# An attention and two-MLP kernel on one core: a split first token block, and low word bits on ScalarE

## The chip, the cores and the metric

The kernel runs on one core of a Trainium2 chip. The metric is device time in microseconds (us), as the median of several runs. The core's engines are called by the names that the profile uses: PE is TensorE's matmul (PEld its weight load), DVE is VectorE, ACT is ScalarE, POOL is GpSimd, and SP is SyncE, which issues the DMA transfers here.

## What is computed

```
# attention: q, k, v float32 [4, 8, 768, 64]; mem_k, mem_v [4, 8, 8, 64]; 24 chunks of 32 queries
k_full = concat(mem_k, k[chunk start - 16 : chunk end + 8])      # clipped at the ends of the sequence
a = exp(s - max(s)),  s = (q_c @ k_full.T) / 8;  a = a / (sum(a) + 1e-9);  out_c = a @ v_full
x = out as [3072 tokens, 512]
# first MLP, weights float64: w_gate, w_val [512, 1536], w_out [1536, 512]
y = (sigmoid(x @ w_gate) * (x @ w_val)) @ w_out
# second MLP, weights float64: w_in [512, 2048], w_out [2048, 512]
h = y @ w_in;  result = (h * sigmoid(1.702 * h)) @ w_out
```

The weights arrive as float64 and are read as pairs of 32-bit words. The two MLPs work with every operand split into a high and a low part in the fp32r format, and each product is the sum of three: high by high, high by low, low by high.

## The kernel before

The 3,072 tokens are worked in six blocks of 512. Attention is cut into 32 tiles of 96 tokens (three chunks each). Tiles 0 to 4 and the first 32 tokens of tile 5 make up block 0; the rest of tile 5 and tiles 6 to 10 (the first 64 tokens of tile 10) make up block 1.

A tile of blocks 0 and 1 goes through these steps, by line: transposes of q and k on PE (L378, L386), copies out of the bank on ACT (L393 to L408), scores on PE (L495), maximum and subtraction on DVE (L512, L515), the exponential on ACT (L523), sum, small add and reciprocal on DVE (L552 to L555), the normalisation into `pw` in three 32-row pieces and one for the memory keys (L563, by DVE or POOL as the list `en` says), transposes of `pw` on PE (L585), copies out on DVE and ACT (L593, L595), the product with v on PE (L645), and last the split into x: the high part `xh` on ACT (L672) and the low part `xl` on DVE (L675). In tiles 0 to 5 (`early`) DVE normalises two pieces and POOL one; in later tiles DVE one and POOL two.

A weight chunk of 128 by 512 is made by `convert`: a 512 KB load, `rebias` on ACT (L257: the high words, scaled, as float32), `rest` on DVE (L262: the low words shifted right by 29), `sign` (the sign bit into the upper half of the low word: on ACT for even chunks, L267, on DVE for odd ones, L271), `join` on DVE (L276), `high` on ACT (L281: the high part of the split) and `low` on POOL (L285). The 36 chunks of the first MLP come first, three per step f (gate, val, out); the 32 chunks of the second MLP come between 600 and 750 us.

For each block the loop over f runs 12 steps: 12 matmuls of the gate (L726 high, L733 low), 12 of val, the gating (sigmoid on ACT L750, product on DVE L753, high part on ACT L756, low part L760), and, one step late, 12 matmuls of the output product (`gemm2`, L897), summed over all steps in four banks. A matmul here has 128 by 128 weights and 512 columns, and each has a weight load of its own.

All instructions are put in order by a planner when the program is written (`Schedule`): each task has an engine, an assumed duration, reads, writes, and a due time that falls back from its successors; at every point the planner takes, for the engine that is free first, the ready task with the earliest due time. Each engine then runs its list strictly in that order. The list `clock` holds the plan's time for products; it begins at 34 us, and tiles 0 to 4 with the first part of tile 5 are due 3 us apart up to that time, while tiles 6 to 10 have no due time of their own.

Of the kernel before, what the change touches and what calls it, by code (L numbers as in the profile page):

```python
# [8 lines left out]
F32 = mybir.dt.float32  # L9
# [3 lines left out]
F16 = mybir.dt.float16  # L13
# [6 lines left out]
CH = 32  # L20
# [102 lines left out]
def c_act(n):  # L123
    return 0.13 + n / 1200.0
# [7 lines left out]
def kernel(  # L132
# [69 lines left out]
    def xkeys(i):  # L202
        return [("x", i, c, o) for c in range(NCH) for o in range(2)]
# [27 lines left out]
    def convert(slot, src, gate=None):  # L231
# [27 lines left out]
        def rest():  # L259

            lo = words()[:, :, 0]
            nc.vector.tensor_scalar(out=lo, in0=lo, scalar1=29, scalar2=None, op0=ALU.logical_shift_right)  # L262

        def sign():

            half = bits().bitcast(F16).rearrange("p (c w) -> p c w", w=4)
            nc.scalar.activation(half[:, :, 1], words()[:, :, 1].bitcast(F32), AF.Copy, scale=2.0**-60)  # L267

        def sign_dve():
            half = bits().bitcast(U16).rearrange("p (c w) -> p c w", w=4)  # L270
            nc.vector.tensor_scalar(  # L271
                out=half[:, :, 1], in0=half[:, :, 3], scalar1=0x8000, scalar2=None, op0=ALU.bitwise_and
            )
# [17 lines left out]
        add("dve", 0.45, rest, r=[kr], w=[kr2])  # L291
        if u % 2:
            add("dve", 0.9, sign_dve, r=[kr], w=[kr2])
        else:
            add("act", 1.4, sign, r=[kr], w=[kr2])
        add("dve", 0.9, join, r=[kr, kr2], w=[kf])
# [38 lines left out]
    held_back = []  # L335
    SL = 0.5

    def attention(t, bufs, banks, pe_path, extra=None):
# [31 lines left out]
        if pe_path:  # L370
# [23 lines left out]

            early = t < NPRO
# [171 lines left out]
        if pe_path:  # L567
# [9 lines left out]
            en = ["dve", "dve" if early else "pool", "pool"]  # L577
            for c in range(NCK):
                tadd(en[c], 0.6 if en[c] == "dve" else 0.95, lambda c=c: ev_norm(c), r=ke + [kk["sm"]], w=[(kk["pw"], c)])
# [73 lines left out]
        def evict(part=None):  # L653

            g = range(t * NCK, (t + 1) * NCK)
            for i, blk in enumerate(sorted({c // NCH for c in g})):
# [7 lines left out]
                due = clock[0] - 3.0 * (NPRO - 1 - t) if t < NPRO and blk == 0 else None  # L664
# [54 lines left out]
    def first_product(slot, xb, n, bk, load=1.0):  # L719
        ts = [slice(t * P, (t + 1) * P) for t in range(NK)]  # L720

        def high():
            w = slots[slot]
            for t in range(NK):
                for x in (xhs, xls):
                    nc.tensor.matmul(  # L726
                        bank[bk][:, :n], w[:, 0, ts[t]], x[xb][:, t, :n], start=t == 0 and x is xhs, stop=False
                    )

        def low():  # L730
            w = slots[slot]
            for t in range(NK):
                nc.tensor.matmul(  # L733
                    bank[bk][:, :n], w[:, 1, ts[t]], xhs[xb][:, t, :n], start=False, stop=t == NK - 1
                )

        product(c_mm(n, 2 * NK), high, [("w", slot, 0)] + xkeys(xb), [("bank", bk)], load)
        product(c_mm(n, NK), low, [("w", slot, 1)] + xkeys(xb), [("bank", bk)], load)
# [46 lines left out]
    pro_banks = [(A0, A1), (Y[0], Y[1]), (Y[2], Y[3]), (G, V), (A0, A1), (Y[0], Y[1])]  # L785
# [104 lines left out]
    def gemm2(b, f, i, n):  # L890
        gh, gl = ghs[i], gls[i]

        def part(wi, g, j):
            def fn():
                w = slots[2 * F1 + f]
                for m in range(NK):
                    nc.tensor.matmul(  # L897
                        bank[Y[m]][:, :n],
                        w[:, wi, m * P : (m + 1) * P],
                        g[:, :n],  # L900
                        start=f == 0 and j == 0,
# [52 lines left out]
    LOAD = 1.12  # L954
    pend = None
    for b in range(NB):
# [5 lines left out]
        for f in range(F1):  # L962
            first_product(f, b % 2, n, G, LOAD)
            i, tail = gated(n, G, 1.0, V, b == 0 or b == NB - 1)
            first_product(F1 + f, b % 2, n, V, LOAD)
            tail()
            if pend:
                gemm2(*pend)
            pend = (b, f, i, n)
# [113 lines left out]
```

## Time and profile before

| what | value |
|---|---|
| median of 3 runs (lowest, highest) | 1261.01 us (1260.43, 1263.02) |
| the profiled execution, its own time | 1264.35 us |
| its span, first to last instruction | 1262.6 us |
| PE busy | 1231.8 us (98%) |
| DVE busy | 620.2 us (49%) |
| ACT busy | 475.0 us (38%) |
| POOL busy | 236.0 us (19%) |
| mean granted clock of TensorE | 0.989 |

The profiled execution took 1264.35 us, of which 1.75 us lie outside the span, and it is 3.3 us above the median of the runs. Busy shares are means over the whole span. A busy PE is one with a matmul under way; matmuls overlap, so that the time from one start to the next says what one costs, and not its own length.

### The profile page before, as it was taken

How to read it: one execution, taken by the hardware profiler on the slowest of the kernel's cores; microseconds unless marked ns; L12 is line 12 of the kernel's file. 1: busy time of each engine (PE TensorE's matmuls, PEld its weight loads, DVE VectorE, ACT ScalarE, POOL GpSimd, SP SyncE). 2: the span in 40 equal slices, each digit the busy share in tenths (PEclk: the TensorE clock that was granted, in tenths of full speed). 3: DMA queues.
4: the chain of work that ended last, by engine and by line, in shares of the span. 5: the costliest groups of instructions: out<-in, count | busy, mean ns of one | idle time of the engine just before them, and what ended most of it. 6: DMA issues, size and time to landing. Idle time of an engine off the chain costs nothing.

```text
span 1262.6 us, 18066 instructions
## 1 busy us (share of the span) xinstructions
PE 1231.8 (98%) x7120; PEld 987.7 (78%) x7120; DVE 620.2 (49%) x1161; ACT 475.0 (38%) x754; POOL 236.0 (19%) x198
## 2 busy tenths in 40 slices
PE   7799899999999999999999999999999999999998
PEld 5677777777777887787788788888888888888886
DVE  6979852786488528816677711122322222222322
ACT  4687742342244224313576632222222222322212
POOL 2465740010000001000365642110010000100000
PEclk9699999999999999999999999999999999999999
DMA  9556522223022202400365410010100200100000
GB/s 205 147 164 179 136 57 67 41 49 69 18 52 49 63 10 49 94 2 18 118 186 157 132 67 1 17 50 1 50 17 1 67 1 1 67 1 1 34 1 34
DMA packets 166036, 78.03 MB, mean 62 GB/s; under 512 B 132542, under 2 KB 153278, under 8 KB 165950
## 3 DMA queue, kind: packets, MB, share of 16 engines
q1 hardware_dynamic: 165950, 76.87, 23.5%
q8 instruction: 56, 0.92, 0.3%
q14 instruction: 30, 0.25, 0.1%
HBM read 64.24 MB, written 12.58 MB: 61 GB/s over the span
## 4 chain that ended last, share of the span: by engine, by line
PE 90%; DVE 5%; DMA 1%; ACT 1%; issue 1%; POOL 1%; SPq 1%; DVEq 0%; POOLq 0%; ACTq 0%
PE bank L726 33%; PE bank L704 21%; PE bank L733 17%; PE bank L897 14%; PE bank L645 2%; PE bank L495 1%; DVE f L276 1%; DVE pw L563 1%; SPq L305 1%; POOL pw_a L563 1%; PE bank L585 0%; DVE raw_s L262 0%; DVE raw L271 0%; DVE raw L262 0%; DVE sm L552 0%
## 5 line engine op out<-in xcount | busy, mean ns | idle before, releaser
L726 PE MATMUL bank<-xh,w 128*128 128x512 f32 x960 | 382.4, 398 | 2.3 <-ACT w L281 2.0
L726 PE MATMUL bank<-xl,w 128*128 128x512 f32 x960 | 380.9, 397 | 0.0
L753 DVE TENSOR_TENSOR sig<-bank,sig 128x512 f32<-128x512 f32 x168 | 115.9, 690 | 434.1 <-ACT sig L750 337.3
L733 PE MATMUL bank<-xh,w 128*128 128x512 f32 x960 | 264.1, 398 | 0.0
L750 ACT ACTIVATE sig<-bank 128x512 f32<-128x512 f32 x168 | 100.6, 599 | 389.6 <-PE bank L733 389.3
L704 PE MATMUL bank<-w,gh 128*128 128x512 f32 x768 | 241.0, 395 | 0.0
L726 PEld LDWEIGHTS bank<-xh,w 128*128 128x128 f32 x960 | 181.5, 189 | 47.9 <-ACT w L281 2.3
L726 PEld LDWEIGHTS bank<-xl,w 128*128 128x128 f32 x960 | 181.5, 189 | 43.3
L733 PEld LDWEIGHTS bank<-xh,w 128*128 128x128 f32 x960 | 179.3, 188 | 42.8
L756 ACT ACTIVATE gh<-sig 128x512 fp32r<-128x512 f32 x168 | 106.2, 632 | 197.4 <-DVE sig L753 190.3
L704 PEld LDWEIGHTS bank<-w,gh 128*128 128x128 f32 x768 | 144.6, 188 | 33.7
L897 PE MATMUL bank<-gh,w 128*128 128x512 f32 x576 | 159.6, 399 | 0.0
L704 PE MATMUL bank<-w,gl 128*128 128x512 f32 x384 | 151.1, 393 | 0.0
L897 PEld LDWEIGHTS bank<-gh,w 128*128 128x128 f32 x576 | 108.5, 190 | 26.5 <-DVE f L918 0.2
L760 DVE TENSOR_TENSOR gl<-sig,gh 128x512 fp32r<-128x512 f32 x128 | 91.0, 711 | 74.5 <-ACT gh L756 74.2
L285 POOL TENSOR_TENSOR w<-f,w 128x512 fp32r<-128x512 f32 x68 | 96.2, 1428 | 62.7 <-ACT w L281 61.1
L563 POOL TENSOR_TENSOR raw<-e,sm 96x448 f32<-96x448 f32 x21 | 21.6, 1029 | 410.8 <-DVE sm L555 410.8
L704 PEld LDWEIGHTS bank<-w,gl 128*128 128x128 f32 x384 | 72.2, 188 | 17.1
L946 POOL TENSOR_TENSOR xl<-f,xh 128x512 fp32r<-128x512 f32 x24 | 31.4, 1318 | 279.9 <-ACT xh L943 279.9
L897 PE MATMUL bank<-gl,w 128*128 128x512 f32 x288 | 79.7, 398 | 0.0
L620 DVE STREAM_TRANSPOSE pt<-raw 32x256 f32<-32x256 f32 x168 | 73.1, 435 | 2.6
L760 POOL TENSOR_TENSOR gl<-sig,gh 128x512 fp32r<-128x512 f32 x40 | 55.7, 1391 | 73.3 <-ACT gh L756 68.7
(84 smaller groups left out, 908.6 us busy)
## 6 DMA issues: line engine op xcount, KB each, us to landing
raw<-in_moe_w_out_dram SPq DMA_DIRECT2D x24, 512.0 KB
raw<-in_moe_w_in_dram SPq DMA_DIRECT2D x16, 512.0 KB
y_dram<-f SPq DMA_DIRECT2D x24, 256.0 KB
f<-y_dram SPq DMA_DIRECT2D x24, 256.0 KB
out_dram<-f SPq DMA_DIRECT2D x23, 256.0 KB
vn<-in_v_dram SPq DMA_DIRECT2D x24, 240.0 KB
raw<-in_moe_w_gate_dram SPq DMA_DIRECT2D x8, 512.0 KB
raw<-in_moe_w_val_dram SPq DMA_DIRECT2D x8, 512.0 KB
```

What stands on the lines that cost most here:

```text
L285: nc.gpsimd.tensor_tensor(out=w[:, 1, :], in0=ft, in1=w[:, 0, :].bitcast(F32), op=ALU.subtract)
L563: eng.tensor_tensor(out=dst, in0=e3()[r, :, c], in1=T["sm"][r].to_broadcast([n, H, keys[1] - keys[0]]), op=ALU.mult)
L620: nc.vector.transpose(T["pt"][r * CH : (r + 1) * CH, :, c * CH : (c + 1) * CH], T["pn"][c * CH : (c + 1) * CH, :, kb * CH : (kb + 1) * CH],)
L704: nc.tensor.matmul(ps_out, a, c, start=(first and i == 0 and j == 0), stop=(last and i == n - 1 and j == 2),)
L726: nc.tensor.matmul(bank[bk][:, :n], w[:, 0, ts[t]], x[xb][:, t, :n], start=t == 0 and x is xhs, stop=False)
L733: nc.tensor.matmul(bank[bk][:, :n], w[:, 1, ts[t]], xhs[xb][:, t, :n], start=False, stop=t == NK - 1)
L750: nc.scalar.activation(sig[:, :n], bank[src_sig][:, :n], AF.Sigmoid, scale=scale)
L753: nc.vector.tensor_tensor(out=sig[:, :n], in0=bank[src_val][:, :n], in1=sig[:, :n], op=ALU.mult)
L756: nc.scalar.activation(gh[:, :n], sig[:, :n], AF.Copy)
L760: eng.tensor_tensor(out=gl[:, :n], in0=sig[:, :n], in1=gh[:, :n].bitcast(F32), op=ALU.subtract)
L897: nc.tensor.matmul(bank[Y[m]][:, :n], w[:, wi, m * P : (m + 1) * P], g[:, :n], start=f == 0 and j == 0, stop=f == F1 - 1 and j == 2,)
L946: nc.gpsimd.tensor_tensor(out=xls[xb][:, m, :], in0=st[:, :BLK], in1=xhs[xb][:, m, :].bitcast(F32), op=ALU.subtract)
```

## The change

The low word bits move to ACT: `rest` becomes an ACT instruction that reads the upper 16 bits of the low word as an unsigned number, scales it by 7.5/65536 and adds 2^23, so that the three bits stand at the foot of the written word. `sign` is now always DVE's, for every chunk, and ACT's form of it goes away. In tiles 0 to 5 DVE normalises one piece and POOL two, as in the later ones. The first block begins with f = 0 and f = 1 for its first 384 tokens (tiles 0 to 3), then does both steps for the other 128 tokens, and goes on with f = 2 at 512. Tiles 0 to 3 are due 3 us apart up to 34 us, tile 4 and the first part of tile 5 at 40 and 46 us, and tiles 6 to 10 are spread over 95 us after that clock value. Tile 5 uses the banks A0 and A1 in place of two of the output's. Some durations that the planner assumes are new.

```diff
 def c_act(n):
-    return 0.13 + n / 1200.0
+    return 0.2 + n / 1100.0
...
-    def xkeys(i):
-        return [("x", i, c, o) for c in range(NCH) for o in range(2)]
+    def xkeys(i, c0=0, n=BLK):
+        return [("x", i, c, o) for c in range(c0 // CH, (c0 + n) // CH) for o in range(2)]
...
         def rest():
-            lo = words()[:, :, 0]
-            nc.vector.tensor_scalar(out=lo, in0=lo, scalar1=29, scalar2=None, op0=ALU.logical_shift_right)
+            half = bits().bitcast(U16).rearrange("p (c w) -> p c w", w=4)
+            nc.scalar.activation(
+                words()[:, :, 0].bitcast(F32), half[:, :, 1], AF.Copy, scale=7.5 * 2.0**-16, bias=2.0**23
+            )
         def sign():
-            half = bits().bitcast(F16).rearrange("p (c w) -> p c w", w=4)
-            nc.scalar.activation(half[:, :, 1], words()[:, :, 1].bitcast(F32), AF.Copy, scale=2.0**-60)
-        def sign_dve():
             half = bits().bitcast(U16).rearrange("p (c w) -> p c w", w=4)
             nc.vector.tensor_scalar(
                 out=half[:, :, 1], in0=half[:, :, 3], scalar1=0x8000, scalar2=None, op0=ALU.bitwise_and
...
-        add("dve", 0.45, rest, r=[kr], w=[kr2])
-        if u % 2:
-            add("dve", 0.9, sign_dve, r=[kr], w=[kr2])
-        else:
-            add("act", 1.4, sign, r=[kr], w=[kr2])
-        add("dve", 0.9, join, r=[kr, kr2], w=[kf])
+        add("act", c_act(512), rest, r=[kr], w=[kr2])
+        add("dve", 0.95, sign, r=[kr], w=[kr2])
+        add("dve", 0.85, join, r=[kr, kr2], w=[kf])
...
+    SPREAD = 95.0
...
-            en = ["dve", "dve" if early else "pool", "pool"]
+            en = ["dve", "pool", "pool"]
             for c in range(NCK):
-                tadd(en[c], 0.6 if en[c] == "dve" else 0.95, lambda c=c: ev_norm(c), r=ke + [kk["sm"]], w=[(kk["pw"], c)])
+                tadd(en[c], 0.75 if en[c] == "dve" else 1.2, lambda c=c: ev_norm(c), r=ke + [kk["sm"]], w=[(kk["pw"], c)])
...
-                due = clock[0] - 3.0 * (NPRO - 1 - t) if t < NPRO and blk == 0 else None
+                due = None
+                if t < 4:
+                    due = clock[0] - 3.0 * (3 - t)
+                elif t < NPRO and blk == 0:
+                    due = clock[0] + 6.0 * (t - 3)
+                elif t < NPE and blk <= 1:
+                    due = clock[0] + SPREAD * (t - NPRO + 1) / (NPE - NPRO)
...
-    pro_banks = [(A0, A1), (Y[0], Y[1]), (Y[2], Y[3]), (G, V), (A0, A1), (Y[0], Y[1])]
+    pro_banks = [(A0, A1), (Y[0], Y[1]), (Y[2], Y[3]), (G, V), (A0, A1), (A0, A1)]
...
+    NEARLY, NFIRST = 2, 4 * TQ
...
-        for f in range(F1):
-            first_product(f, b % 2, n, G, LOAD)
-            i, tail = gated(n, G, 1.0, V, b == 0 or b == NB - 1)
-            first_product(F1 + f, b % 2, n, V, LOAD)
+        steps = [(f, 0, n) for f in range(F1)]
+        if b == 0:
+            steps[:NEARLY] = [(f, c, m) for c, m in ((0, NFIRST), (NFIRST, n - NFIRST)) for f in range(NEARLY)]
+        for f, c0, m in steps:
+            first_product(f, b % 2, m, G, LOAD, c0)
+            i, tail = gated(m, G, 1.0, V, b == 0 or b == NB - 1)
+            first_product(F1 + f, b % 2, m, V, LOAD, c0)
             tail()
             if pend:
                 gemm2(*pend)
-            pend = (b, f, i, n)
+            pend = (b, f, i, m, c0)
```

`first_product` and `gemm2` take the first column `c0` and write or read the columns from there on.

## Rows read from the trace of the kernel before

**Rows 1.** Stretches: length; busy us of PE, PEld, DVE, ACT, POOL; clock; DMA share, GB/s.

```profile
...
0.00:49.17 49.17, 32.00 (x481) 26.52 (x481) 37.56 (x79) 23.54 (x51) 14.22 (x23) 0.85 0.68 146
49.17:54.88 5.71, 5.71 (x14) 4.45 (x14) 5.68 (x6) 3.59 (x6) 4.21 (x3) 0.50 1.13 285
...
49.17:187.35 138.18, 128.77 (x852) 101.72 (x853) 109.93 (x160) 99.98 (x156) 84.96 (x70) 0.95 0.57 151
187.35:1262.00 1074.65, 1071.08 (x5789) 859.48 (x5787) 472.72 (x924) 351.52 (x548) 136.81 (x105) 1.00 0.18 47
...
```

**Rows 2.** Waits of TensorE (PE), 49.17 to 187.35 us: total us, times, longest.

```profile
...
PE bank L585 <- POOL pw_a L563: 6.2, 3, 3.2
...
```

**Rows 3.** VectorE (DVE) in order of time, 27 to 49 us: start, length, instruction.

```profile
...
27.74 1.89 DVE L563 TENSOR_TENSOR pw<-e,sm 32x448 f32<-32x448 f32 x2
...
43.34 0.76 DVE L262 TENSOR_SCALAR raw<-raw 128x512 int32<-128x512 int32 x2
...
44.88 0.73 DVE L271 TENSOR_SCALAR raw<-raw 128x512 uint16<-128x512 uint16 x1
...
48.72 0.69 DVE L276 SCALAR_TENSOR_TENSOR f<-f,raw 128x512 int32<-128x512 int32 x1 [0.26 <-ACT raw L267]
...
```

**Rows 4.** PE in order of time: pieces between 49 and 185 us.

```profile
...
49.17 0.79 PE L726 MATMUL bank<-xh,w 128*128 128x512 f32 x1 [2.04 <-ACT w L281]
49.76 0.63 PE L726 MATMUL bank<-xl,w 128*128 128x512 f32 x1
...
54.02 0.63 PE L726 MATMUL bank<-xl,w 128*128 128x512 f32 x1
...
81.19 0.88 PE L645 MATMUL bank<-pt,vn 128*64 128x96 f32 x16
...
86.21 0.60 PE L386 MATMUL bank<-ident_a,qkn_a 128*128 128x128 f32 x4
...
102.87 0.88 PE L585 MATMUL bank<-ident_a,pw_a 96*128 96x96 f32 x8 [1.20 <-POOL pw_a L563]
...
182.69 0.39 PE L726 MATMUL bank<-xh,w 128*128 128x512 f32 x1
...
184.32 0.40 PE L726 MATMUL bank<-xl,w 128*128 128x512 f32 x1
...
```

**Rows 5.** DVE by line and shape, 0 to 49.17 us: busy us, mean ns, idle before.

```profile
...
L563 DVE TENSOR_TENSOR pw<-e,sm 32x448 f32<-32x448 f32 x12 | 10.7, 893 | 0.3
L512 DVE TENSOR_REDUCE mx<-bank 96x4 f32<-96x256 f32 x12 | 4.7, 411 | 2.5 <-PE bank L495 2.4
L515 DVE TENSOR_TENSOR e<-bank,mx 96x256 f32<-96x256 f32 x12 | 4.5, 412 | 0.1
L552 DVE TENSOR_REDUCE sm<-e 96x8 f32<-96x512 f32 x6 | 4.0, 674 | 0.0
...
```

**Rows 6.** The same view for GpSimd (POOL).

```profile
...
L563 POOL TENSOR_TENSOR pw<-e,sm 32x448 f32<-32x448 f32 x6 | 7.0, 1170 | 28.3 <-ACT qt L393 13.1 <-DVE sm L555 10.1 <-DVE sm L554 5.2
...
```

**Rows 7.** Groups of DVE by line and shape, 49.17 to 187.35 us.

```profile
...
L262 DVE TENSOR_SCALAR raw<-raw 128x512 int32<-128x512 int32 x21 | 17.6, 844 | 5.6 <-DMA raw<-in_moe_w_out_dram 5.1 <-DMA raw<-in_moe_w_val_dram 0.6
L262 DVE TENSOR_SCALAR raw_s<-raw_s 128x512 int32<-128x512 int32 x10 | 12.9, 1290 | 0.0
L271 DVE TENSOR_SCALAR raw<-raw 128x512 uint16<-128x512 uint16 x11 | 12.1, 1097 | 0.1
...
L271 DVE TENSOR_SCALAR raw_s<-raw_s 128x512 uint16<-128x512 uint16 x5 | 5.7, 1139 | 0.1
...
```

**Rows 8.** The same view and stretch for ScalarE (ACT).

```profile
...
L267 ACT ACTIVATE raw<-raw 128x512 f16<-128x512 f32 x10 | 13.7, 1371 | 0.0
L257 ACT ACTIVATE f<-raw 128x512 f32<-128x512 f32 x21 | 13.6, 671 | 0.0
...
```

**Rows 9.** DVE in order of time, at 78.76 us.

```profile
...
78.76 2.77 DVE L262 TENSOR_SCALAR raw_s<-raw_s 128x512 int32<-128x512 int32 x1
```

**Rows 10.** POOL in order of time, at 77.44 us.

```profile
...
77.44 2.55 POOL L285 TENSOR_TENSOR w<-f,w 128x512 fp32r<-128x512 f32 x2
...
```

More of the change, by code (lines that the diff above doesn't have):

```diff
@@ L12 @@
 I64 = mybir.dt.int64
-F16 = mybir.dt.float16
 U16 = mybir.dt.uint16
@@ L393, in ev_q @@
                 nc.scalar.activation(T["qt"].rearrange("p a b -> p (a b)"), b0[:, : NP * TQ], AF.Copy)
-            early = t < NPRO
             def ev_k():
@@ L717, in product, with first_product @@
         clock[0] += dur * load
-    def first_product(slot, xb, n, bk, load=1.0):
+    def first_product(slot, xb, n, bk, load=1.0, c0=0):
         ts = [slice(t * P, (t + 1) * P) for t in range(NK)]
@@ L726, in high @@
                     nc.tensor.matmul(
-                        bank[bk][:, :n], w[:, 0, ts[t]], x[xb][:, t, :n], start=t == 0 and x is xhs, stop=False
+                        bank[bk][:, :n], w[:, 0, ts[t]], x[xb][:, t, c0 : c0 + n], start=t == 0 and x is xhs, stop=False
                     )
@@ L733, in low @@
                 nc.tensor.matmul(
-                    bank[bk][:, :n], w[:, 1, ts[t]], xhs[xb][:, t, :n], start=False, stop=t == NK - 1
+                    bank[bk][:, :n], w[:, 1, ts[t]], xhs[xb][:, t, c0 : c0 + n], start=False, stop=t == NK - 1
                 )
-        product(c_mm(n, 2 * NK), high, [("w", slot, 0)] + xkeys(xb), [("bank", bk)], load)
-        product(c_mm(n, NK), low, [("w", slot, 1)] + xkeys(xb), [("bank", bk)], load)
+        product(c_mm(n, 2 * NK), high, [("w", slot, 0)] + xkeys(xb, c0, n), [("bank", bk)], load)
+        product(c_mm(n, NK), low, [("w", slot, 1)] + xkeys(xb, c0, n), [("bank", bk)], load)
     ng = [0]
@@ L888, in attention_b, with gemm2 @@
             attention(t, x, (A0, A1), False, (0 if head else NCK, 2 - t % 2 if head else 0, first or t % TPB == 0))
-    def gemm2(b, f, i, n):
+    def gemm2(b, f, i, n, c0):
         gh, gl = ghs[i], gls[i]
@@ L897, in fn @@
                     nc.tensor.matmul(
-                        bank[Y[m]][:, :n],
+                        bank[Y[m]][:, c0 : c0 + n],
                         w[:, wi, m * P : (m + 1) * P],
                         g[:, :n],
-                        start=f == 0 and j == 0,
+                        start=f == 0 and j == 0 and c0 == 0,
                         stop=f == F1 - 1 and j == 2,
```

## Prediction

> **What bounds the kernel now.** I read the stretches first, then TensorE's waits, then the order of instructions around the first product. From 187.35 us to the end TensorE is busy 1,071.1 of 1,074.7 us at full clock; before that it is busy 128.8 of 138.2 us, and in the first 49.17 us only 32.0 of 49.2 [rows 1]. So nothing is to be had behind 187 us: each product there must be done in any case, and no edit changes their number. What the change gains or loses, it gains or loses before 187 us, and it then arrives at the end unaltered.
>
> The start comes at 49.17 us with the first matmul of the gate, which waited for ACT's high part of the first weight chunk, and that for DVE's `join` at 48.72 us [rows 3, 4]. DVE was busy 37.6 of the 49.2 us [rows 1]. So the first product waits for a DVE that is behind with tiles 0 to 5 and gets to the first weights last.
>
> From 49.17 to 187.35 us two things are lost on PE. It idles 138.18 - 128.77 = 9.4 us, of which 6.2 us wait for POOL's normalisation of tiles 6 to 10 [rows 1, 2]. And the mean granted clock is 0.95, which costs 0.05 x 138.2 = 6.9 us [rows 1]. At the lower level (1.2 GHz) the first matmuls stand (54.02 - 49.76) / 10 = 0.426 us apart, at the higher level (2.4 GHz) (184.32 - 182.69) / 7 = 0.233 us [rows 4]. The lower level in the first 5.7 us of the products, where the granted clock is 0.50 [rows 1], costs half of them, 2.9 us, and comes again after any early start, since PE works here on many small matmuls with gaps. The other 4.0 us of the clock loss follow PE's gaps. So 9.4 + 4.0 = 13.4 us could at best come back.
>
> **The start (-11 us, between -5 and -16).** The first product no longer needs tiles 4 and 5, whose due times now lie behind it. On DVE one tile costs, for norm, maximum, subtraction and sum alone, (10.7 + 4.7 + 4.5 + 4.0) / 6 = 4.0 us [rows 5], so 8.0 us for two, and their copies and low parts come on top; I take 10. Tiles 0 to 3 lose one of DVE's two norms each; a pair takes 1.89 us and DVE's mean is 0.89 [rows 3, 5], so about 0.9 x 4 = 3.6 us. The three `rest` before the start (0.76 us for two) go to ACT, and the first chunk's `sign` comes to DVE for 0.73 [rows 3]: nothing to speak of. On the other side POOL now has two norms of 1.17 us in a row per tile [rows 6], 1.2 us more in each tile's chain, and fewer tiles are there to fill DVE's gaps. With all 10 + 3.6 + about 2 us of later conversions moved behind the start it would come at some 33 us, which is the best end, -16. If half of it goes into gaps it is some 41. I take 38, that is -11; the bad end is -5.
>
> One rule speaks against the norm's move. `rest` takes 0.38 us alone (0.76 for two), and 2.77 us when it is issued at 78.76 us while POOL runs from 77.44 to 79.99 [rows 3, 9, 10]. The Trainium skill's page SBUF — State Buffer, section "Who interferes with whom", says that VectorE and GpSimd share one pair of ports as an exclusive lock, for VectorE's fast modes and for its instructions with two SBUF inputs, and that the second to come stands still. By that rule the trace agrees, and four more POOL norms of 1.17 us before the start could hold DVE for up to 4.7 us; the start would be worth -6 and the sum below -4, still inside the forecast's own range.
>
> **Tiles 4 and 5 under the products (+3 us, between 0 and +4).** Their `pw` transposes and products with v, 0.88 us each at full clock [rows 4], fall behind the start: 2 x 1.76 = 3.5 us of PE, less what fits a gap.
>
> **The split (+8 us, between 0 and +17).** Two steps of 36 matmuls with 512 columns become 72 with 384 and 72 with 128. No product of another width than 512 stands in the trace. If the time went by columns alone, the split would be free; if each piece cost the full 0.233 us, it would cost 72 x 0.233 = 16.8 us. The nearest row of 128 columns with a 128 by 128 weight load is the transpose at L386: 0.60 us for four, 0.15 us each [rows 4], in another number format and with the drain of the last one in it. For 384 I take 0.20, between three quarters of 0.233 (0.175) and all of it. A pair then costs 0.35, that is 0.117 more than 0.233, and 72 of them 8.4 us. The gating adds two more rounds of sigmoid, product and split at smaller widths, on engines with room at that point.
>
> The Trainium skill's page TensorE: Matmul & The Clock Gate, section "Back-to-back issue gap", gives about 81 ns for a load and matmul pair of 128 columns in a stream. By that, as an estimate, the pair would be 0.28 us, the split 3.4 us and the sum about -14, on the side of the first rival; no run here shows it for this number format.
>
> **Stalls behind the start (-9 us, between -2 and -13).** In the second stretch 31 conversions stand in the rows. Their `rest` takes 17.6 + 12.9 = 30.5 us of DVE, and 16 `sign` take 12.1 + 5.7 = 17.8 us, 1.11 each [rows 7]. Without `rest` and with 15 more `sign` (16.7 us) DVE has 13.8 us less to do, of 109.9 [rows 1]. Per chunk the chain from load to PE shortens on DVE from about 2.4 to 2.0 us, and the weights and tiles get ahead of PE, the more so as PE spends longer on the split steps. The waits for POOL's norms of tiles 6 to 10 are not touched themselves, but these tiles get due times of their own and a planner that assumes 1.2 us and not 0.95 for such a norm, so that the transposes should stand later in PE's order. Nothing but the plan says so; hence two thirds of 13.4 us, and not all.
>
> ACT gets `rest` for 33 chunks and gives up 16 `sign` at 1.37 us, 21.9 us [rows 8]. `rebias`, which reads the same words at the same stride, takes 0.67 us [rows 8]; at that price `rest` costs 22.1 us, and ACT's load stays at 100 of 138 us. The other end is the price of the old `sign`, 1.37, which touches two-byte words as `rest` does. I take 0.67, because `rest` writes four-byte words and only the writer of two-byte words is slow here; this is the open point of a rival below. The conversions of the second MLP fall in the stretch in which PE never waits; their cover is PE's own work.
>
> **The sum.** 1264.35 - 11 + 3 + 8 - 9 = 1255.4 us for an execution like the profiled one, which stands 3.3 us above the median; so 1252 us for the median. This is a gain of 0.7%; from 0.2% on (2.5 us) a difference can be told here.
>
> **Rivals.**
> *The split is nearly by columns and PE runs on without stalls*: 384 columns cost 0.175 us, and 128 cost the transpose without its drain (a matmul of 512 lasts 0.40 us and the next starts after 0.233, so 0.17 is drain, and (0.60 - 0.17) / 4 = 0.11 [rows 4]). A pair is 0.285 us, the split 3.7 us, and -14 + 3 + 4 - 12 = -19 gives 1242 us. For it speaks that a load of weights is hidden behind 512 columns; against it, that 6.2 of 9.4 idle us hang on norms which the change leaves alone.
> *Each piece costs like 512 columns*, because the weight load and not the columns sets the pace: -11 + 3 + 17 - 9 = 0, 1261 us. For it speaks that 0.233 us is more than half of 0.426, so something beside the clock is in it [rows 4].
> *The start is given back*: PE comes to the 128-token steps and tiles 4 and 5 aren't there. Some 60 matmuls of 0.20 us and 2.9 us at the lower level take PE from 38 to 53 us; DVE has 10 us for these tiles and three more chunks at 2.0 us, 16 us, which ends at 54. Another chunk or two before them and PE stands 8 us: 1260 us.
> *ACT becomes the bound, and the kernel slower*: `rest` costs 1.37 us. ACT's load from the start to 187 us goes from 100 to 100 - 21.9 + 33 x 1.37 = 123 us. DVE, which set the pace before, was filled 109.9 / 138.2 = 0.80; at that filling ACT would need 123 / 0.80 = 154 us in place of 138, and with the start's 11 us the sum is +5: 1266 us. It decides from 1.23 us for `rest` on, where (78.1 + 33 x 1.23) / 0.80 = 148 us uses up the early start.
>
> **How the numbers follow.** Forecast 0.42 (own range 1247 to 1257), cheap split without stalls 0.18, split at full price 0.17, start given back 0.10, ACT-bound 0.13. The range from 1239 to 1266 leaves out the far ends of the bounds: -16 + 0 + 0 - 13 would give 1232, and -5 + 4 + 17 - 2 would give 1275. Faster takes the forecast but for 0.02, the cheap split, and 0.02 from each of the next two: 0.62. Same: 0.02 of the forecast, 0.11 of the full price and 0.05 of the lost start, 0.18. Slower is the rest, 0.20.
>
> **What the profile after would show.** The first L726 matmul near 38 us, and not 49; pieces of 384 columns some 0.20 us apart and of 128 some 0.15; `rest` on ACT at 0.67 us; DVE with about 14 us less to do before block 1; PE's idle time behind the start near 3 us and a clock above 0.95. The prediction is wrong if the 128-column pieces stand 0.2 us apart or more, if PE waits long ahead of them, or if ACT's high parts are what PE waits for all through block 0.

## The result, and the profile after

The changed kernel takes 1269.50 us as the median of four runs (1267.71 to 1271.40), against 1261.19 us before (1260.43 to 1263.02): a ratio of 1.0062 [1.0045, 1.0079], slower by 0.6%. The forecast was 1252 us, the range 1239 to 1266. The profiled execution took 1267.71 us, the shortest of its four, and that of before 1264.35, more than any of its timed ones; so the two traces differ by 3.4 us where the medians differ by 8.3; the other 4.9 us are in no trace here. From 800 to 1200 us, where TensorE is never idle and its granted clock is 1.00 throughout, the profiled executions of before, e4, e9, e13 and e16 get through 1722 matmuls and the thirteen others through 1728 or 1729, whatever the edit, so that some 2 us between two executions say nothing about two kernels.

First the waits of TensorE over the whole span, after (total us, times, longest):

```profile
PE bank L578 <- POOL pw L556: 10.2, 2, 8.4
PE bank L373 <- DMA qn<-in_q_dram: 10.1, 2, 5.3
PE bank L578 <- POOL pw_a L556: 5.9, 1, 5.9
```

Then TensorE in order of time, after (L578 transposes `pw`, L638 is the product with v, L898 is `gemm2`):

```profile
36.58 1.54 PE L578 MATMUL bank<-ident,pw 96*128 96x96 f32 x8 [8.40 <-POOL pw L556]
...
51.52 0.44 PE L726 MATMUL bank<-xh,w 128*128 128x384 f32 x1 [0.96 <-ACT xh L672]
52.74 0.52 PE L726 MATMUL bank<-xl,w 128*128 128x384 f32 x1 [0.78 <-DVE xl L675]
...
58.77 0.34 PE L726 MATMUL bank<-xl,w 128*128 128x384 f32 x1
...
59.83 0.34 PE L726 MATMUL bank<-xl,w 128*128 128x384 f32 x1
60.12 0.88 PE L578 MATMUL bank<-ident,pw 96*128 96x96 f32 x8
60.78 0.94 PE L733 MATMUL bank<-xh,w 128*128 128x384 f32 x4
...
63.05 0.88 PE L638 MATMUL bank<-pt,vn 128*64 128x96 f32 x16
63.86 0.97 PE L733 MATMUL bank<-xh,w 128*128 128x384 f32 x4
...
66.94 0.27 PE L726 MATMUL bank<-xh,w 128*128 128x128 f32 x1
...
68.05 0.28 PE L726 MATMUL bank<-xh,w 128*128 128x128 f32 x1
...
170.21 1.09 PE L733 MATMUL bank<-xh,w 128*128 128x512 f32 x4
177.22 1.54 PE L578 MATMUL bank<-ident_a,pw_a 96*128 96x96 f32 x8 [5.92 <-POOL pw_a L556]
179.46 1.55 PE L638 MATMUL bank<-pt,vn 128*64 128x96 f32 x16 [0.70 <-ACT w L278]
180.93 1.98 PE L898 MATMUL bank<-gh,w 128*128 128x512 f32 x4
182.75 0.39 PE L726 MATMUL bank<-xh,w 128*128 128x512 f32 x1
182.98 0.39 PE L726 MATMUL bank<-xl,w 128*128 128x512 f32 x1
```

The first product comes at 51.52 us, not 38 and not 49.17 [rows 4]. The last two rows are the second block's first product: block 0 has 12 steps with 4 + 4 `xl` matmuls, and the one at 182.98 us is the first after their columns are done. Before, the same place looked like this (TensorE in order of time):

```profile
176.19 0.88 PE L645 MATMUL bank<-pt,vn 128*64 128x96 f32 x16 [1.23 <-ACT pt L595]
177.00 1.20 PE L897 MATMUL bank<-gh,w 128*128 128x512 f32 x4
178.03 0.39 PE L726 MATMUL bank<-xh,w 128*128 128x512 f32 x1
178.26 0.39 PE L726 MATMUL bank<-xl,w 128*128 128x512 f32 x1
```

So the second block began 4.7 us later than before, and TensorE's last matmul ends 1079.1 us behind that point (1080.4 before). Between the first product and that point the stretches tell two stories; first after (the last two rows are the parts of the second), then before (columns as in [rows 1]):

```profile
51.52:170.00 118.48, 117.00 (x876) 96.91 (x877) 98.25 (x131) 91.10 (x162) 74.13 (x66) 0.99 0.59 159
170.00:182.98 12.98, 6.37 (x36) 4.94 (x34) 6.06 (x14) 3.19 (x7) 5.65 (x6) 0.74 0.22 35
170.00:177.22 7.22, 1.30 (x7) 0.73 (x5) 3.50 (x6) 1.03 (x2) 3.78 (x4) 0.90 0.22 34
177.22:182.98 5.76, 5.06 (x30) 4.21 (x30) 2.57 (x8) 2.16 (x5) 1.86 (x2) 0.53 0.23 36
```

```profile
49.17:170.00 120.83, 112.66 (x767) 88.75 (x768) 104.14 (x148) 94.79 (x147) 77.93 (x63) 0.95 0.61 166
170.00:178.26 8.26, 7.03 (x48) 5.64 (x47) 4.26 (x10) 4.55 (x8) 4.86 (x6) 1.00 0.22 35
```

Up to 170 us TensorE loses 1.5 us idle and 0.01 x 118.5 = 1.2 us of clock, 2.7 in all, where before it lost 8.2 + 6.0 = 14.2: a gain of 11.5 us. Behind 170 us it loses 6.6 idle. A low clock costs only what TensorE does in it: up to 177.22 us it is idle for 5.9 of the 7.2 us, and from there the clock costs 0.47 x 5.06 = 2.4. That is 9.0 in all, where before it lost 1.2: 7.8 us given back. In that place it waits for tile 10, the last of block 1. VectorE and GpSimd there, after, in order of time:

```profile
171.41 0.69 DVE L753 TENSOR_TENSOR sig<-bank,sig 128x512 f32<-128x512 f32 x1 [1.68 <-PE bank L733]
172.01 0.30 DVE L452 STREAM_TRANSPOSE f<-f 128x128 f32<-128x128 f32 x1
172.24 0.64 DVE L545 TENSOR_REDUCE sm<-e 96x8 f32<-96x512 f32 x1
172.91 1.21 DVE L547 TENSOR_SCALAR sm<-sm 96x8 f32<-96x8 f32 x1
174.16 0.20 DVE L548 RECIPROCAL sm<-sm 96x8 f32<-96x8 f32 x1
174.40 0.61 DVE L556 TENSOR_TENSOR pw_a<-e,sm 32x448 f32<-32x448 f32 x1
```

```profile
174.51 2.66 POOL L556 TENSOR_TENSOR pw_a<-e,sm 32x448 f32<-32x448 f32 x3 [0.40 <-DVE sm L548]
```

Tile 10's exponentials end at 170.40 us; its row sums stand in VectorE's list behind a product that waits 1.68 us for TensorE. The second block reads tile 10's tokens, and the last two chunks' slots share memory with `pw_a` and its inputs; what follows in TensorE's list needs one or the other.

### The profile page after: what moved, and what is told of

Same layout as the page of the kernel before. It is cut to its first block, busy times and chain, and to the rows that moved or that the text cites. A ratio compares the mean times of both kernels' runs of the same rounds, so it can differ in the third digit from the quotient of the medians.

```text
span 1265.9 us, 18240 instructions
## 1 busy us (share of the span) xinstructions
PE 1228.2 (97%) x7192; PEld 990.8 (78%) x7192; DVE 622.5 (49%) x1123; ACT 476.2 (38%) x792; POOL 242.0 (19%) x206
## 4 chain that ended last, share of the span: by engine, by line
PE 93%; DVE 3%; SPq 1%; POOL 1%; DMA 1%; issue 1%; ACT 0%; DVEq 0%; POOLq 0%; ACTq 0%
PE bank L726 35%; PE bank L704 21%; PE bank L733 18%; PE bank L898 16%; PE bank L638 2%; PE bank L488 1%; SPq L299 1%; DVE f L273 1%; DVE raw L268 1%; DMA qn<-in_q_dram 0%; PE bank L373 0%; PE bank L578 0%; PE bank L381 0%; POOL pw_a L556 0%; DVE e L508 0%
## 5 line engine op out<-in xcount | busy, mean ns | idle before, releaser
L726 PE MATMUL bank<-xl,w 128*128 128x512 f32 (+2 forms) x976 | 384.7, 395 | 0.8 <-DVE xl L675 0.8
L726 PE MATMUL bank<-xh,w 128*128 128x512 f32 (+2 forms) x976 | 382.9, 393 | 2.1 <-ACT sig L750 1.1
L753 DVE TENSOR_TENSOR sig<-bank,sig 128x512 f32<-128x512 f32 (+2 forms) x170 | 116.2, 684 | 439.9 <-ACT sig L750 336.8
L733 PE MATMUL bank<-xh,w 128*128 128x512 f32 (+2 forms) x976 | 264.4, 395 | 0.0
L750 ACT ACTIVATE sig<-bank 128x512 f32<-128x512 f32 (+2 forms) x170 | 100.8, 593 | 387.1 <-PE bank L733 386.8
L704 PE MATMUL bank<-w,gh 128*128 128x512 f32 x768 | 238.3, 391 | 0.0
L726 PEld LDWEIGHTS bank<-xh,w 128*128 128x128 f32 x976 | 184.3, 189 | 44.8 <-ACT sig L750 2.2
L726 PEld LDWEIGHTS bank<-xl,w 128*128 128x128 f32 x976 | 184.2, 189 | 44.6 <-DVE xl L675 1.0
L733 PEld LDWEIGHTS bank<-xh,w 128*128 128x128 f32 x976 | 180.6, 188 | 41.9
L756 ACT ACTIVATE gh<-sig 128x512 fp32r<-128x512 f32 (+2 forms) x170 | 106.7, 627 | 197.1 <-DVE sig L753 189.6
L898 PE MATMUL bank<-gh,w 128*128 128x512 f32 (+2 forms) x592 | 160.1, 393 | 0.0
L898 PEld LDWEIGHTS bank<-gh,w 128*128 128x128 f32 x592 | 110.1, 189 | 25.7 <-issue 0.2
L282 POOL TENSOR_TENSOR w<-f,w 128x512 fp32r<-128x512 f32 x68 | 94.7, 1399 | 60.6 <-ACT w L278 60.2
L898 PE MATMUL bank<-gl,w 128*128 128x512 f32 (+2 forms) x296 | 80.4, 393 | 0.0
L273 DVE SCALAR_TENSOR_TENSOR f<-f,raw 128x512 int32<-128x512 int32 x56 | 69.9, 1250 | 10.3 <-ACT f L256 7.6
L613 DVE STREAM_TRANSPOSE pt<-raw 32x256 f32<-32x256 f32 x168 | 73.2, 435 | 2.6
```

Source lines behind the costliest of these rows:

```text
L273: nc.vector.scalar_tensor_tensor(out=fi, in0=fi, scalar=3, in1=words()[:, :, 0], op0=ALU.logical_shift_left, op1=ALU.bitwise_or)
L282: nc.gpsimd.tensor_tensor(out=w[:, 1, :], in0=ft, in1=w[:, 0, :].bitcast(F32), op=ALU.subtract)
L613: nc.vector.transpose(T["pt"][r * CH : (r + 1) * CH, :, c * CH : (c + 1) * CH], T["pn"][c * CH : (c + 1) * CH, :, kb * CH : (kb + 1) * CH],)
L704: nc.tensor.matmul(ps_out, a, c, start=(first and i == 0 and j == 0), stop=(last and i == n - 1 and j == 2),)
L726: nc.tensor.matmul(bank[bk][:, :n], w[:, 0, ts[t]], x[xb][:, t, c0 : c0 + n], start=t == 0 and x is xhs, stop=False)
L733: nc.tensor.matmul(bank[bk][:, :n], w[:, 1, ts[t]], xhs[xb][:, t, c0 : c0 + n], start=False, stop=t == NK - 1)
```

## The experiments

The table puts the sixteen runs beside the two kernels: the second matmul (`xl`) of the first product; tile 6's first transposes; tile 10's `pw` transposes; the `xl` matmul with which the second block begins (B); from there to TensorE's end, all us of the profiled execution (in e4 and e7 the slowest of all, 4.6 and 5.5 us above the median); the median, and the ratio to the runs of the kernel before on the same chip.

| run | first | tile 6 | tile 10 | B | to end | median | ratio |
|---|---|---|---|---|---|---|---|
| before | 49.8 | 57.9 | 174.1 | 178.3 | 1080.4 | 1261.2 | 1 |
| after | 52.7 | 70.6 | 177.2 | 183.0 | 1079.1 | 1269.5 | 1.0062 [1.0045, 1.0079] |
| e1 | 48.9 | 59.8 | 166.0 | 172.8 | 1079.2 | 1258.8 | 0.9988 [0.9978, 0.9998] |
| e2 | 48.8 | 64.6 | 175.2 | 178.8 | 1079.9 | 1264.5 | 1.0037 [1.0022, 1.0051] |
| e3 | 64.9 | 69.9 | 180.1 | 184.2 | 1080.5 | 1271.4 | 1.0094 [1.0079, 1.0109] |
| e4 | 49.4 | 78.7 | 194.3 | 200.3 | 1083.4 | 1284.8 | 1.0198 [1.0158, 1.0238] |
| e5 | 44.9 | 71.0 | 172.9 | 178.4 | 1080.0 | 1264.2 | 1.0028 [1.0016, 1.0040] |
| e6 | 49.9 | 54.3 | 169.1 | 179.6 | 1078.1 | 1262.2 | 1.0008 [0.9998, 1.0017] |
| e7 | 56.8 | 65.1 | 182.6 | 186.8 | 1079.1 | 1266.1 | 1.0039 [1.0017, 1.0061] |
| e8 | 47.9 | 55.0 | 178.4 | 184.1 | 1078.0 | 1268.7 | 1.0061 [1.0043, 1.0078] |
| e9 | 46.3 | 62.6 | 174.0 | 179.2 | 1082.9 | 1267.8 | 1.0050 [1.0035, 1.0065] |
| e10 | 49.3 | 55.4 | 177.5 | 181.6 | 1078.1 | 1265.0 | 1.0033 [1.0021, 1.0045] |
| e11 | 44.6 | 63.2 | 174.4 | 180.4 | 1080.1 | 1266.3 | 1.0045 [1.0028, 1.0061] |
| e12 | 48.3 | 67.4 | 174.8 | 180.8 | 1079.4 | 1267.5 | 1.0047 [1.0032, 1.0062] |
| e13 | 53.7 | 71.5 | 177.2 | 183.0 | 1081.7 | 1269.4 | 1.0051 [1.0035, 1.0067] |
| e14 | 49.5 | 58.4 | 169.4 | 174.0 | 1078.2 | 1259.7 | 0.9978 [0.9968, 0.9988] |
| e15 | 52.3 | 70.2 | 173.2 | 187.1 | 1081.1 | 1275.4 | 1.0111 [1.0095, 1.0128] |
| e16 | 52.2 | 70.1 | 173.3 | 178.4 | 1083.9 | 1268.7 | 1.0060 [1.0046, 1.0074] |

### The start: e2, e3, e5

The three edit the changed kernel. e2 puts the second early norm back on VectorE; e3 takes the split away; e5 makes the loads of tiles 4 and 5 follow tile 3's, because the trace shows tile 4 loaded and worked on second.

```diff
-            en = ["dve", "pool", "pool"]                                  # e2
+            en = ["dve", "dve" if t < NPRO else "pool", "pool"]
-            steps[:NEARLY] = [(f, c, m) for c, m in ((0, NFIRST), ...     # e3
+            pass
+        if t in (4, 5):                                                   # e5
+            pre = pre + [(pro_bufs[3].k["vn"], 0)]
```

> The changed kernel with two of the three norms of tiles 0 to 5 on DVE again. Theory B: POOL's run of norms before the start shrinks from 9.5 to some 5 us, the first product starts at 46 us or before, the time falls by 5 us or more to 1264 or less. Theory A: tile 4 still comes second, the first product stays near 50 us and the time above 1266.

> The changed kernel with all of block 0 at 512 columns. In the trace the split costs 72 x (0.177 + 0.112 - 0.233) = 4.0 us of PE. If the early pieces bought no start (theory A, the start is late for another reason), the first product moves to some 55 us, as tiles 4 and 5 are needed then, and the time is between 1265 and 1272. If the split is the whole loss, the time falls by 4 us or more.

> The changed kernel, with the loads of tiles 4 and 5 made to wait in the list until tile 3's have been issued, so that the six tiles are loaded in the order 0 to 5. Theory (the start is late because tile 4 is loaded and worked on second, ahead of tiles 1 to 3): the first gate product at or before 46 us (51.5 in the changed kernel) and the time at or below 1264 us. Rival (the start waits for the norms that now lie on GpSimd, whatever the order of the tiles): the first product at 49 us or later, the wait of TensorE for pw at 8 us or more, and the time 1267 to 1271 us.

e5 brought the first product to 44.34 us and e2 to 45.40 (its second matmul waited until 48.82), as their theories had said, and both times stand just above the 1264 us that these named; e3's time is as expected. So the order of the tiles and the norms on GpSimd each made the start late. How the delay divides these runs do not show: in e1 and e12, which edit neither directly, the first product comes sooner too, at 48.45 and 47.30 us. GpSimd before the start, after (in order of time), and VectorE beside it:

```profile
33.18 9.48 POOL L556 TENSOR_TENSOR pw<-e,sm 32x448 f32<-32x448 f32 x9 [0.40 <-DVE sm L548]
```

```profile
40.98 4.74 DVE L268 TENSOR_SCALAR raw<-raw 128x512 uint16<-128x512 uint16 x2
```

Three tiles' norms stand in a row there, and two `sign` take 4.74 us in place of some 1.5. But the table's first column says little of the time: starts from 44.6 to 64.9 us lead to second blocks between 173 and 187 us (e4's at 200) in no order. e3 starts 12 us later than the changed kernel and ends 2 us later.

### The conversion: e4, e8, e12

e4 undoes the change's conversion of the words alone; e8 is the kernel before with that conversion alone; e12 moves the low parts of the first 36 chunks from GpSimd to VectorE.

```diff
-        add("pool", c_pool(512), low, r=[kf, ("w", slot, 0)], w=[("w", slot, 1)])     # e12
+        add("dve" if u < NW else "pool", c_dve(512) if u < NW else c_pool(512), low, ...
-            nc.gpsimd.tensor_tensor(out=w[:, 1, :], in0=ft, ...
+            (nc.vector if u < NW else nc.gpsimd).tensor_tensor(out=w[:, 1, :], in0=ft, ...
```

> The changed kernel with the low word bits on DVE and the sign shared by ACT and DVE as before. Theory C (DVE got no relief, since what it waits for POOL moves from the instruction taken away to those that stay: conversions hold DVE 86.8 us before and 86.2 after): the time stays within 4 us of 1269.5 and the conversions hold DVE for 82 to 92 us. Rival (the relief is real and hidden by other losses): the conversions hold DVE for 95 us or more, and the time rises by 5 us or more.

> The kernel before with only the conversion of the weights changed (low word bits on ScalarE, sign bits on VectorE). Theory (VectorE is held by the port it shares with GpSimd, so the instructions that stay take up the time of those that go): within 0.4% of before, 1256 to 1266 us, and the conversions hold VectorE for the same 86 us up to 187 us. Rival (the 15 us that the undone conversion cost the changed kernel is what the new conversion is worth anywhere): 1250 us or less.

> The changed kernel with the weights' low parts of the first triple of products (the 36 subtractions of 1.3 us and more on GpSimd) moved to VectorE. Theory (the sign and the join of the weights take 1.4 and 1.2 us instead of 0.74 and 0.69 because they stand still while GpSimd works): with GpSimd nearly idle between 60 and 170 us their means there fall below 0.9 and 0.85 us, and the three conversions together hold VectorE for less than the two do now (86 us). Rival (they are slow by their own strides, or by ScalarE's transfers): the means stay above 1.2 and 1.0 us, VectorE is full, and the time rises above 1280 us.

Undone, the conversion costs the changed kernel 15 us (10 to 20 by e4's runs, which lie between 1279.6 and 1289.4); done alone, it costs the kernel before 7. Both theories missed in time, and so did e8's rival. In a third pair, e9 and e1 below, undoing it costs some 8 to 9. So it has no one price. What goes with the gain or the loss is tile 10, which the new conversion brings 17 and 8 us forward in the changed kernel and in e1, and puts 4 us back in e8; why, no run here shows. Groups of VectorE by line and shape up to 190 us, after and then e12 (L268 `sign`, L273 `join`, L282 `low`):

```profile
L268 DVE TENSOR_SCALAR raw<-raw 128x512 uint16<-128x512 uint16 x24 | 33.4, 1425 | 0.1
L273 DVE SCALAR_TENSOR_TENSOR f<-f,raw 128x512 int32<-128x512 int32 x24 | 29.8, 1241 | 3.8 <-ACT f L256 3.2
```

```profile
L282 DVE TENSOR_TENSOR w<-f,w 128x512 fp32r<-128x512 f32 x36 | 26.9, 755 | 1.1 <-ACT w L278 1.0
L268 DVE TENSOR_SCALAR raw<-raw 128x512 uint16<-128x512 uint16 x24 | 21.3, 887 | 4.3 <-ACT raw L262 4.3
L273 DVE SCALAR_TENSOR_TENSOR f<-f,raw 128x512 int32<-128x512 int32 x24 | 19.1, 799 | 1.2 <-ACT f L256 1.1
```

With GpSimd's subtractions gone, the same `sign` falls from 1425 to 887 ns and the same `join` from 1241 to 799, as the theory had said. By the Trainium skill's rule (SBUF — State Buffer, section "Who interferes with whom"), cited with the prediction, the trace agrees: VectorE's instructions got shorter when GpSimd's went.

Summed over all shapes, the conversion holds VectorE 87.2 us before (90 instructions), 87.0 after (72) and 88.8 in e12 (108; the theory had said less than 86). That the first two are alike does not need the rule: at their undisturbed prices, 0.38 us for a `rest` and 0.73 for a `sign` [rows 3], the 36 `rest` that go and the 18 `sign` that come are 13.7 and 13.1 us, an even exchange. Nor is the sum fixed: the same 72 instructions hold VectorE 76.4 us in e2 and 88.4 in e8.

### The row of tiles 6 to 10: e1, e6, e7, e9, e10, e11

Tiles 6 to 10 pass one after another through the banks A0 and A1. The change puts tile 5 there as well, and tile 6 starts at 70.6 us instead of 57.9.

```diff
-    pro_banks = [..., (A0, A1), (A0, A1)]          # e1, e6, e9, e11
+    pro_banks = [..., (A0, A1), (Y[0], Y[1])]
-    SPREAD = 95.0                                  # e7
+    SPREAD = 75.0
+                if NPRO <= t < NPE and blk <= 1:   # e10, in the kernel before
+                    due = clock[0] + 95.0 * (t - NPRO + 1) / (NPE - NPRO)
```

> The changed kernel with tile 5 on the banks Y0 and Y1 again, so that it no longer follows tile 4 through A0 and A1. Theory A (the shared banks put tile 4, which must leave them before tile 5, ahead of tiles 1 to 3 in every list, and that is why the first product starts at 51.5 us): tile 4 goes behind tile 1, the first product starts before 46 us, and the time falls by 5 to 10 us to some 1261. Theory B (POOL's second norm is the cause: its nine norms in a row from 33 to 43 us): the first product stays at 49 us or later and the time within 3 us of 1269.5. Against A in either case: the output products of f = 0 then need Y0 and Y1, and wait for tile 5.

> The changed kernel with tile 5 in its own two banks and with the second early norm back on VectorE, that is the edits of the two earlier runs together. Theory (two causes that add up): the first product at 43 to 45 us and the time at or below 1257 us. Rival (both edits only spare one and the same wait, that for tile 10 later on): no better than the banks alone, 1258 to 1262 us.

> The changed kernel with the constant that spreads tiles 6 to 10 over the first block at 75 in place of 95, so that tile 10 is due some 20 us earlier. Theory (what was won by 170 us is given back because tile 10 comes too late): no wait of TensorE for pw_a above 2 us, and the time 1262 to 1265 us. Rival (bringing the tiles forward takes VectorE's time from the conversions, so that products wait for those): 1268 us or more, with the waits on the weights longer.

> The changed kernel with the old conversion of the weights (as in the earlier run that took 1284.8 us) and with tile 5 in its own two banks. Theory (the time is set by when tile 10, the last of the tiles that pass one after another through the banks A0 and A1, ends; the undone conversion cost so much because that row of tiles ended at 194 us; tile 6 can start some 11 us earlier with tile 5 out of these banks): the first transpose of tile 10's products (pw) at 180 to 186 us and the time 1268 to 1277 us. Rival (the old conversion costs its 15 us in the products of the first block themselves): 1280 us or more, whatever tile 10 does.

> The kernel before with one edit of the change alone: the due times that spread tiles 6 to 10 over the first block. Theory (these due times draw the row of tiles together, from 116 us between tile 6's start and tile 10's last transposes to about 106): tile 10's transposes before 170 us instead of 174.1, no wait there, and 1257 to 1260 us. Rival (the tiles only push the conversions back, so what they win is lost on the weights): 1261 us or more.

> The changed kernel with both repairs: the loads of tiles 4 and 5 behind tile 3's, and tile 5 in its own two banks. Theory (the start and the end of the row of tiles are two separate losses): the first product at 45 us or earlier, tile 10's transposes at 168 us or earlier, and 1254 to 1258 us. Rival (both repairs only bring tile 10 forward): 1258 to 1260 us, as with the banks alone.

e1 alone repairs the change: tile 6 at 59.8 us, tile 10 at 166.0, the second block at 172.8, 10.2 us sooner than in the changed kernel, and the median is 10.7 lower. The time is what theory A had named, but not by its route, an early start; that start came at 48.45 us. TensorE in order of time, e1:

```profile
166.01 0.82 PE L578 MATMUL bank<-ident_a,pw_a 96*128 96x96 f32 x8
...
169.59 0.88 PE L638 MATMUL bank<-pt,vn 128*64 128x96 f32 x16
...
172.37 0.40 PE L726 MATMUL bank<-xh,w 128*128 128x512 f32 x1
172.79 0.50 PE L726 MATMUL bank<-xl,w 128*128 128x512 f32 x1
```

Tile 10's rows carry no wait, and products stand between them. e9 has the same edit with the old conversion: tile 10 comes at 174.0 us in place of e4's 194.3, and the time falls from 1284.8 to 1267.8 us, 12 to 22 us by e4's runs, for one line about banks (tile 10 came 6 us ahead of the theory's 180 to 186). The others missed their theories: e6 and e10 have about their rivals' times, e7 lies between the two, e11 above both. e6's tile 10 was in time, but the second block came 10.5 us behind it, so there the products were the later. In e7 the shorter spread held up tiles 0 to 5. In e10 the due times drew tile 6 forward but tile 10 back. e11 started at 44.6 us and had the banks, and its tile 10 still came at 174.4. How long the row takes, from 102 us (e5) to 123 (e8), I cannot derive from any one edit.

### Tile 10 alone: e13, e15, e16

These leave the changed kernel's order as it is up to some 162 us and move only tile 10's steps forward in the finished list, by hand. The diff is e16's core; e13 and e15 pull the sums otherwise and leave `xl` where it was.

```diff
-        for i in order:
+        for i in self.fix(order, T):
...
+        pull(k, 1)                      # key transposes, one place earlier on PE
+        pull(s, 3)                      # scores, three places
+        for i in dve[:4]: pull(i, 0)    # maxima, subtractions: right behind the scores
+        pull(h["act", "ev_exp"][0], 1)
+        pull(dve[4], 2)                 # row sums, ahead of the product with the sigmoid
+        # then: norms, pw transposes and copies right behind what they read;
+        # xl on DVE ahead of the transposes that wait for the next tiles' loads
```

> The changed kernel, the same instructions and the same orders up to 162 us; only tile 10's own steps stand further forward on their engines: its key transposes one place and its scores three places earlier on TensorE, its row maxima, exponentials, sums and norms ahead of the conversion, the sigmoid and the product they stood behind. Theory (the second block's first product reads tile 10's tokens; it came at 182.98 us in the changed kernel, and from it to TensorE's end are 1078 to 1083 us in every run so far): that product at 177 to 180 us, the wait for pw_a at most 2.5 us, and 1263 to 1266 us. Rival (tile 10 is only seen waiting, and what holds the stage are the last weights or the products' own pace): the wait goes elsewhere, the product stays at 182 us or later, 1267 to 1271 us.

> As the run before it with tile 10 moved, and now tile 10's sum, reciprocal and norms stand ahead of the last join and of the product with the sigmoid on VectorE, and ahead of the clearing of the raw buffers on GpSimd; in that earlier run the sum still stood behind the product (172.66 us), which waited for TensorE, so the norms began no sooner (174.4 us in both) and the second block's first product came at 183.00 us. Theory (that product follows tile 10): norms from about 171.5 us on, the wait for pw_a at most 2 us, the product at 178.5 to 180.5 us and the time 1264 to 1267 us. Rival (tile 10 only goes with another limit): the product at 182 us or later and 1268 to 1271 us.

> As the two runs before it with tile 10 moved; the last join and the clearing of the raw buffers stay ahead of tile 10's sums, as in the changed kernel, so the loads of the next tiles are not late, and tile 10's low parts (xl) now stand on VectorE ahead of the transposes that wait for those loads (in the run before, xl stood behind them until 186.6 us and the second block's first product waited 6.3 us for it, so its second matmul came at 187.07 us and the time was 5.9 us above the changed kernel's). Theory (the time follows the second block's first product, and that follows tile 10): pw transposes at 173 to 174 us, the product at 177 to 180 us, 1263 to 1267 us. Rival (other limits hold the stage, and tile 10 only goes with them): the product at 182 us or later, 1268 us or more.

e13 failed as a test: the sums stayed behind the product with the sigmoid, and tile 10 and the second block came as in the changed kernel, so that the rival's numbers, which it has, decide nothing. e15 brought tile 10 to 173.2 us, but its norms now stood ahead of GpSimd's clearing of the load buffers, the next tiles' loads came late, and `xl` stood on VectorE behind a transpose that waits for them. TensorE in order of time, e15 (lines 28 higher):

```profile
180.10 0.63 PE L754 MATMUL bank<-xh,w 128*128 128x512 f32 x1
187.07 0.80 PE L754 MATMUL bank<-xl,w 128*128 128x512 f32 x1 [6.34 <-DVE xl L703]
```

The second block began 4.1 us later than in the changed kernel, and the median rose by 5.9. e16 mends that (lines 39 higher):

```profile
173.31 0.88 PE L617 MATMUL bank<-ident_a,pw_a 96*128 96x96 f32 x8 [2.24 <-POOL pw_a L595]
...
178.39 0.50 PE L765 MATMUL bank<-xl,w 128*128 128x512 f32 x1
```

With nothing but tile 10 moved, the second block begins 4.6 us sooner, as the theory said. The median, 1268.69 us, does not follow; it is the rival's. From B to the end this execution takes 4.9 us longer than the changed kernel's. Two of them go in a stall between 190 and 200 us (PE busy 8.10 of 10, after 10.00): `gemm2` waits for the first block's output to be copied out of its banks, and the copies wait for a store.

```profile
198.83 0.50 PE L937 MATMUL bank<-gh,w 128*128 128x512 f32 x1 [1.27 <-ACT f L960]
199.21 0.69 DVE L958 COPY f<-bank 128x512 f32<-128x512 f32 x1 [8.31 <-DMA y_dram<-f]
```

Another two lie behind 740 us, in the difference between executions that the result names. So e16 shows that tile 10 moves B; it does not show what moving B alone is worth at the end.

### Both repairs at once: e14

e1's banks and e12's subtractions on VectorE.

> The changed kernel with tile 5 in its own two banks and the low parts of the first weights on VectorE. Theory (two things bound the second block's first product: tile 10, which tile 5's banks bring to 166 us, and the pace of the first block's products, which the low parts on VectorE brought from 72.5 to 67.6 us behind an unbroken stream at 150 us): the product at 168 to 172 us and 1249 to 1257 us, below both kernels. Rival (VectorE is too full, so tiles 6 to 10 slow down and tile 10 is late again): 1259 us or more.

The second block began at 174.0 us, and the time is 1259.67 us, 0.9978 [0.9968, 0.9988] of the kernel before: 0.2% faster than that kernel and 0.8% than the changed one, but not to be told from e1, and 2.7 us above the theory's upper end. The time is the rival's, though not for its reason: tile 10, at 169.4 us, was not late again. At 150 us the products stood 72.3 us behind an unbroken stream (the time less 0.233 us for every 512 columns done), where e1 had 73.2 and e12 67.6; so e12's gain before 150 us did not come along with the banks.

## Why the prediction was wrong

**The start: -11 us predicted, +2.4 measured.** The step that failed is "the first product no longer needs tiles 4 and 5, whose due times now lie behind it". A due time is not a place in the list: tile 6 and the memory that opens behind the early tiles have due times too, tile 4 was loaded second and worked on ahead of tiles 2 and 3, and only tile 5's last steps (60.12 and 63.05 us) fell behind the start. With the order forced (e5) the start was 4.8 us early, the bad end of my bounds. The second step, 3.6 us off VectorE by the moved norm, was a loss: with the norm back (e2) the first product came 6.1 us sooner. Of the 8.40 us that TensorE waits before 36.58 us some 3.4 are these norms, from 33.18 us on; until then they themselves waited for VectorE's sums of three tiles.

**Tiles under the products: +3 predicted, 1.5 measured**, for the one tile that went there: (60.78 - 60.12) + (63.86 - 63.05).

**The split: +8 predicted, 4.0 measured.** Pieces of 384 columns stand (59.83 - 58.77) / 6 = 0.177 us apart and of 128 columns (68.05 - 66.94) / 10 = 0.111; 72 x (0.177 + 0.111 - 0.233) = 4.0 us. The first rival's prices (0.175 and 0.11) were right and mine too large; the rival at full price is out. The Trainium skill's 81 ns for a pair of load and matmul at 128 columns (TensorE: Matmul & The Clock Gate, section "Back-to-back issue gap") is less than the 111 measured here for fp32r.

**`rest` on ACT: 0.67 us predicted, 0.667 measured**; the ACT-bound rival is out. ACT by line and shape, 51.52 to 190 us, after:

```profile
L262 ACT ACTIVATE raw<-raw 128x512 f32<-128x512 uint16 x19 | 12.7, 667 | 2.1 <-DMA raw<-in_moe_w_out_dram 2.1
```

**Stalls behind the start: -9 predicted; -11.5 up to 170 us, then +7.8, so -3.7.** The reason given for it, 13.8 us less work on VectorE, did not appear (87.2 to 87.0 us of conversion), and the prediction's own rows say why: it priced the 31 `rest` that go and the 15 `sign` that come at their means under GpSimd's work, 0.98 and 1.11 us. At the undisturbed 0.38 and 0.73 of [rows 3] they are 11.8 and 11.0 us, and the exchange frees 0.8. What the trace shows in its place is that up to 170 us TensorE no longer waits for the norms of tiles 6 to 9. That these tiles' own due times did it was not shown alone: in e10 they did not help the kernel before.

The terms add up: +2.4 + 1.5 + 4.0 - 11.5 + 7.8 = +4.2 us at the second block, where the traces show +4.7 and the forecast had -9. By size the start is the step that failed: it missed by 13.4 us, the stalls by 5.3 the same way, while the two prices were too high by 5.5.

**The step that decided** is the forecast's logic that whatever is gained before 187 us "then arrives at the end unaltered", so that the terms may be added. A gain arrives only if the second block's first product is earlier, and that needs tile 10: e5 and e11 began their first product 4.8 and 6.5 us sooner than the kernel before, and their medians are 1264 and 1266 us. The kernel before waited 1.23 us for tile 10 and was all but tied: the prediction had the waits on `pw_a` in its rows and took them for a loss to be won back, not for a second bound with no room. In 16 of the 18 kernels B comes 3.7 to 6.8 us behind tile 10's transposes, whatever the start was, and TensorE ends 1078 to 1084 us behind B. That the bank line made tile 10 late is shown by e1, and by e9 against e4. That tile 10's place moves B is shown by e16; that e16's 4.6 us reach the end is not, beyond the agreement of the other runs, whose medians lie 1079 to 1089 us behind B (e16's 1090). What sets the length of the row of tiles stays open, and with it why the new conversion costs 7 us in one kernel and saves 15 in another; of the medians' 8.3 us, the 4.9 that the traces do not show stay open too. No rival named this: "the start is given back" put the loss at the 128-token steps, where TensorE did not wait.

## What to carry to other kernels

Before adding up what a stage can win, look for a second chain that ends where the stage ends, and ask how much room it has; a wait of 1 us on it says that there is none. An edit that looks like bookkeeping (which bank, which due time) can lengthen that chain by more than the edits one is costing. Where an instruction runs beside another engine's work, its mean is not its own price: what taking it away frees is nearer to its undisturbed time, which some row of the same trace shows. With a planner, forecast a place in the list only from the list, since due times of other tasks reach back through shared memory and banks.

## What the runs showed of the hardware

While GpSimd works on two-input instructions, VectorE's instructions stretch: with 36 subtractions of GpSimd gone (e12) the same `sign` fell from 1425 to 887 ns and the same `join` from 1241 to 799, and 108 conversion instructions held VectorE about as long as 72 in the changed kernel, 88.8 and 87.0 us. In this fp32r stream a matmul with its own weight load costs 0.111 us at 128 columns, 0.177 at 384 and 0.233 at 512 at full clock, so the short pieces cost less than the prediction took (0.15 and 0.20). In the 5.9 us wait that ends at 177.22 us the granted clock fell; its mean is 0.53 from there to 182.98 us, against 1.00 from 170 to 178.26 us in the kernel before.
